# Windowed attention beside a channel MLP: which engine empties three PSUM tiles at the end of a pair of fill jobs

## The chip, the cores and the metric

The kernel runs on one core of one Trainium2 chip. The metric is the device time of one execution in microseconds (us). Before the change it is 768.82 us, the median of three runs (768.52 to 769.15).

## The reference, cut to what matters

```python
def _A_ref(x, wqkv, wo):                       # x: 1 x 2048 x 512, 32 heads of 16, window 256
    q, k, v = heads(x @ wqkv)
    scores = einsum("bhqd,bhkd->bhqk", q, k) * 16 ** -0.5
    scores = where((i >= j) & (i - j < 256), scores, -1e9)
    return merge(einsum("bhqk,bhkd->bhqd", softmax(scores), v)) @ wo
def _B_ref(x, w1, b1, w2, b2):                 # w1: 512 x 1792, w2: 1792 x 512
    return gelu(layernorm(x) @ w1 + b1) @ w2 + b2
xn = layernorm(x)
return x + _A_ref(xn, wqkv, wo) * silu(_B_ref(xn, w1, b1, w2, b2))
```

All of it is fp32. The projections and the MLP are made from a high and a low half of each operand, in three matmuls (`PASSES`).

## The kernel before

**The steps.** The 32 heads are worked on in 8 groups of 4, the 2048 tokens in 16 blocks of 128. One step `t` of the main loop (-16 to 128) works on block `t % 16` of group `t // 16`. The change touches steps 14 to 115. TensorE (PE) issues in each of these:

1. scores of four heads into the PSUM tile `stb`, first half (`prob_block(..., 1)`). ScalarE (ACT) takes their exponentials into a tile `pt`, and GpSimd (POOL) masks `pt`.
2. scores of the block that is 12 steps ahead, for its row maxima, into `xy` and, where the block has two blocks before it, into `zo` (`max_block`). VectorE (DVE) then merges `zo` into `xy` (COPY_PREDICATED) and reduces `xy` to the maxima `mt` (TENSOR_REDUCE).
3. some fill matmuls into the two PSUM tiles `fb0` and `fb1` (`fill_in(t, 0)`).
4. scores of the other half into `stb` (`prob_block(..., 0)`), and ACT's exponentials of these. `stb` is one tile, so this waits for the exponentials of item 1.
5. more fill matmuls (`fill_in(t, 1)`).
6. probabilities times values for the block of the step before, 12 narrow matmuls at most (24 in the profile, which has two rows for each), into `otb`, a quarter of the second bank of the tile `zo` (`pv_step`). `otb` is then copied to a quarter of the SBUF tile `oraw`. A full `oraw` goes to memory.

**The fill jobs.** Work that the later groups and the MLP need (the q and k projection of a group, the values' projection, the first MLP layer) runs as fills. `tandem` runs two such jobs at once through the two halves of TensorE's rows. One sums into `fb0`, the other into `fb1`, over steps `t0` to `t1`. In step `t1`, which this document calls a closing step, `fb0` is copied by ACT and `fb1` by DVE, into a tile `pjr` (projections), `vt` (values) or `hr` (MLP). The next pair starts in the next step and writes the same two tiles. There are 19 closing steps handled by the dictionary `closing`: 12 with `pjr`, 4 with `vt`, 3 with `hr`. (Pairs that end before step 9 or after step 115 go another way and are not touched.)

**The order.** `nc` is a wrapper that keeps each engine's instructions in the order in which the code issues them. So the order of the calls in the main loop is the order on every engine, and the engines meet through semaphores only. A tile is tracked as a whole where its PSUM bank is shared: the next step's scores into `zo` wait until `otb` has been copied.

```python
closing[t1] = (one[2], (fb[0], t1, nc.scalar.copy)), (two[2], (fb[1], t1, nc.vector.tensor_copy))   # L455, in tandem
```

Of the kernel before, what the change touches and what calls it, by code (L numbers as in the profile page):

```python
# [18 lines left out]
P = 128  # L19
# [30 lines left out]
def mixer_kernel(ctx, tc, x, wqk, wv, wo, w1, b1, w2, b2, out):  # L50


    nc = SimpleNamespace(**{name: Ordered(tc, name) for name in ("tensor", "vector", "scalar", "gpsimd", "sync")})
# [99 lines left out]
    def run(steps):  # L153
        for step in steps:
            step()
# [13 lines left out]
    def open_slot(i):  # L169
        slots.append(bigp.tile([P, 2, 2, S], F32R, tag=f"qk{i}", name=f"qk{i}"))  # L170
# [16 lines left out]
    otb = zo[:, 1, 256:384]  # L187
# [93 lines left out]
    closing = {}  # L281
# [191 lines left out]
    def max_block(n, qb):  # L473

        slot = slots[n % 2]
        if qb % 4 == 0:
            mts[n, qb // 4] = small.tile([P, 2, 2, 4], F32, tag="mt", name=f"mt_{n}_{qb}")
        lo = max(qb - 1, 0)
        off = 128 * (lo + 1 - qb)

        def scores(p, a, first):
            r = slice(64 * a, 64 * a + 64)
            out, keys = ((zo[:, a, P * p: P * (p + 1)], slice(P * (qb - 2), P * (qb - 1))) if first else
                         (xy[:, a, 256 * p + off: 256 * (p + 1)], slice(P * lo, P * (qb + 1))))
            nc.tensor.matmul(out, slot[r, 0, p, P * qb: P * (qb + 1)], slot[r, 1, p, keys], start=True, stop=True)

        for p, a, first in ((0, 1, False), (0, 0, False), (1, 1, False), (1, 0, False),
                            (0, 1, True), (0, 0, True), (1, 1, True), (1, 0, True)):
            if qb >= 2 or not first:
                scores(p, a, first)  # L490
        four = xy.rearrange("q a (p k) -> q a p k", p=2)
        nc.vector.copy_predicated(four[:, :, :, 128:256], mask,
                                  neg if qb < 2 else zo[:, :, 0:256].rearrange("q a (p k) -> q a p k", p=2))
        nc.vector.tensor_reduce(out=mts[n, qb // 4][:, :, :, qb % 4],
                                in_=four[:, :, :, off:256],
                                axis=AX.X, op=ALU.max, negate=True)

    def max_rows(n, c, t):

        mt = mts.pop((n, c))  # L500
        mh = small.tile([P, 2, 2, 2, 4], F32R, tag="mh", name=f"mh_{n}_{c}")
        nc.vector.tensor_copy(mh[:, :, 0], mt)
        nc.vector.tensor_sub(mh[:, :, 1], mt, mh[:, :, 0].bitcast(F32))
        mT = small.tile([P, 32], F32, tag="mT", name=f"mT_{n}_{c}")
        nc.vector.transpose(mT, mh.rearrange("p a l i b -> p (a l i b)").bitcast(F32))
        rows = mT_d[n, c]
        at(t + 1, nc.sync.dma_start, rows.rearrange("r (i t) -> i r t", i=4), mT)
        behind(t + 2, nc.sync.dma_start, slots[n % 2][3:P:32, 0, :, 512 * c: 512 * (c + 1)].bitcast(F32),
               rows.rearrange("(h p b) t -> h p (b t)", h=4, p=2))
# [4 lines left out]
    def prob_block(n, kb, p):  # L514
        slot = slots[n % 2]
        w = min(384, S - P * kb)
        pt = pp.tile([P, 2, 384], F32, tag="pt", name=f"pt_{n}_{kb}_{p}")
        both = xy if p and 16 * n + kb + LEAD >= 16 * NQ else stb[0]
        for a in (1, 0):
            r = slice(64 * a, 64 * a + 64)  # L520
            nc.tensor.matmul(both[:, a, 0:w], slot[r, 1, p, P * kb: P * (kb + 1)],
                             slot[r, 0, p, P * kb: P * kb + w], start=True, stop=True)
        nc.scalar.activation(pt[:, :, 0:w], both[:, :, 0:w], AF.Exp, scale=DH ** -0.5)
        nc.gpsimd.affine_select(out=pt[:, :, 0:P], in_=pt[:, :, 0:P], pattern=[[0, 2], [1, P]],
                                compare_op=ALU.is_ge, fill=0.0, base=0, channel_multiplier=-1)
        if w == 384:
            nc.gpsimd.affine_select(out=pt[:, :, 256:384], in_=pt[:, :, 256:384],
                                    pattern=[[0, 2], [-1, P]], compare_op=ALU.is_gt, fill=0.0,
                                    base=0, channel_multiplier=1)
        pts[(n, kb, p)] = pt  # L530


    outs = {}

    def pv_step(n, qb):

        lo = max(qb - 2, 0)
        for kb in range(lo, qb + 1):
            for j in range(4):
                nc.tensor.matmul(otb[32 * j: 32 * j + DH + 1], vt[:, kb, (4 * n + j) % 16],  # L540
                                 pts[n, kb, j // 2][:, j % 2, P * (qb - kb): P * (qb - kb + 1)],
                                 start=(kb == lo), stop=(kb == qb),
                                 skip_group_check=True, tile_position=(0, 32 * j))
        if qb % 4 == 0:
            outs[0] = sgp.tile([P, 512], F32, tag="or", name=f"oraw_{n}_{qb}", bufs=2)
        by = nc.vector.tensor_copy if 16 * n + qb + 1 in closing else nc.scalar.copy
        by(outs[0][:, P * (qb % 4): P * (qb % 4 + 1)], otb)
        if qb % 4 == 3:
            (at if n or qb > 7 else behind)(16 * n + qb + 2, nc.sync.dma_start, oT_d[n // 2, n % 2::2, :, P * (qb - 3): P * (qb + 1)], outs[0])

# [81 lines left out]
    def at(t, fn, *args):  # L632
        plan.setdefault(t, []).append((fn, args))
# [40 lines left out]
    n, raw = raws["qk"]  # L674
# [104 lines left out]
    def fill_in(t, half):  # L779
        now[:] = t, half  # L780
        run(delayed.pop((t, half), ()))
        for fn, args in fills.get((t, half), ()):
            fn(*args)

    end = 16 * NQ
    for t in range(-16, end + 1):
        m = t + LEAD
        if t == -5:
            open_slot(1)
            for k in range(4):  # L790
                at(-4 + k, clear_part, k)
        if 0 <= t < end:
            if t == 0:
                early.close()
                stb.append(attn.enter_context(tc.tile_pool(name="ps_s2", bufs=1, space=PSUM)).tile(
                    [P, 2, 512], F32, name="stb"))
            prob_block(t // 16, t % 16, 1)
        if t >= 0 and m < end:
            max_block(m // 16, m % 16)
        fill_in(t, 0)  # L800
        for fn, args in plan.get(t, []):
            fn(*args)
        if 4 <= m < LEAD:
            max_block(0, m)
        if 0 <= t < end:
            prob_block(t // 16, t % 16, 0)
        fill_in(t, 1)
        if 0 <= m < 4:
            max_block(0, m)
        if t >= 1:  # L810
            pv_step((t - 1) // 16, (t - 1) % 16)
        for fn, args in closing.get(t, ()):
            fn(*args)
        run(lns.get(t, ()))
        if 0 <= m < end and m % 4 == 3:
            max_rows(m // 16, m % 16 // 4, t)
        for fn, args in ends.get(t, []):
            fn(*args)
# [20 lines left out]
    for f in range(6, NF, 2):  # L839
        t = gp.tile([P, 2, 512], F32, tag="ohl", name=f"hr_{f}", bufs=4)  # L840
# [421 lines left out]
```

## Time and profile before

| what | value |
|---|---|
| median of three runs | 768.82 us |
| the profiled execution: its time, its span | 768.78 us, 767.1 us |
| granted TensorE clock | 0.999 |
| busy time of DVE, ACT, POOL | 529.1, 433.3, 292.6 us |
| copies of `otb` to `oraw` by ACT, by DVE | 109, 19 |
| steps that the change touches | between about 110 and 414 us of the span |

How to read it: "PE" is TensorE's matmuls, "PEld" its weight loads, which run ahead of the matmuls. [...] In the lists by time, the columns are the start and the duration in us, the engine, the line (the wrapper's line 42 for all), the operation, what it writes and reads, its shape, and in brackets the engine's idle time before it with what ended that. [...] In a row of a tile, three durations are the shortest, the median and the longest in ns.

### The profile page before, as it was taken

To read this page: it belongs to the slowest core of one execution; us is meant where nothing else is said; L and a number is where in the kernel's file an instruction comes from. 1 tells how busy PE (TensorE), PEld (TensorE's weight loads), DVE (VectorE), ACT (ScalarE), POOL (GpSimd) and SP (SyncE) were. 2 spreads that over 40 slices of the span, in tenths; PEclk is the share of its full clock that TensorE was granted. 3 is DMA by queue.
4 is the path that set the end of the run, shared out by engine and by line. 5 is a ranking of instruction groups with operands and counts; after the bars stand their busy time and mean duration, and the time that the engine had idled before them with its cause. 6 is when DMAs were issued, how large, how long until landed. Compare 5 with 4: busy or idle time off the path is not lost.

```text
span 767.1 us, 18795 instructions
## 1 busy us (share of the span) xinstructions
PE 746.9 (97%) x7428; PEld 583.6 (76%) x7428; DVE 529.1 (69%) x852; ACT 433.3 (56%) x723; POOL 292.6 (38%) x595
## 2 busy tenths in 40 slices
PE   9999999999999999999999999999999999999997
PEld 8777676666768887676676688888878888888886
DVE  6786777877777778897874447763657665676473
ACT  7736767867666666677776755444645553442001
POOL 7613556666565554766766800030101100001102
PEclk9999999999999999999999999999999999999999
DMA  7623455645447862455734283541202222253531
GB/s 261 207 45 78 94 133 138 153 112 134 95 100 227 241 199 98 113 147 144 201 111 152 61 289 121 180 151 54 70 29 93 99 87 84 77 165 116 173 96 55
DMA packets 56951, 99.40 MB, mean 130 GB/s; under 512 B 11104, under 2 KB 11360, under 8 KB 56864
## 3 DMA queue, kind: packets, MB, share of 16 engines
q1 hardware_dynamic: 56864, 98.21, 44.4%
q8 instruction: 58, 0.95, 0.5%
q14 instruction: 29, 0.24, 0.1%
HBM read 51.39 MB, written 29.62 MB: 106 GB/s over the span
## 4 chain that ended last, share of the span: by engine, by line
PE 81%; DVE 8%; issue 3%; ACT 3%; POOL 3%; DMA 2%; SPq 0%; DVEq 0%; ACTq 0%; POOLq 0%
PE acc L42 19%; PE fb L42 16%; PE zo L42 12%; PE p L42 9%; PE stb L42 6%; PE h L42 6%; PE s L42 6%; PE xy L42 4%; DVE xy L42 2%; DMA qk<-pjr 2%; PE pv L42 2%; ACT pt L42 2%; DVE mt L42 2%; POOL pt L42 1%; DVE pjr L42 1%
## 5 line engine op out<-in xcount | busy, mean ns | idle before, releaser
L42 POOL TENSOR_SCALAR_AFFINE_SELECT pt<-pt 128x256 f32<-128x256 f32 x480 | 193.2, 427 | 162.6 <-ACT pt L42 160.8
L42 ACT ACTIVATE pt<-stb 128x768 f32<-128x768 f32 (+1 forms) x244 | 188.6, 773 | 73.1 <-PE stb L42 64.9
L42 DVE TENSOR_REDUCE mt<-xy 128x4 f32<-128x1024 f32 (+1 forms) x128 | 152.6, 1192 | 4.4
L42 PE MATMUL acc<-w,gh 128*128 128x512 f32 x432 | 134.7, 393 | 0.0
L42 DVE COPY_PREDICATED xy<-upper,zo 128x512 f32<-128x512 int32 x112 | 77.5, 692 | 67.0 <-PE zo L42 66.5
L42 PE MATMUL fb<-xnT,wqb 64*128 64x512 f32 (+1 forms) x684 | 117.4, 406 | 2.9 <-DVE pjr L42 1.3
L42 PE MATMUL zo<-pt,vt 128*17 128x128 f32 x2880 | 103.7, 275 | 1.7 <-DVE xy L42 1.2
L42 POOL TENSOR_TENSOR xo<-xo,gated 128x512 f32<-128x512 f32 x15 | 20.2, 1348 | 219.1 <-DVE gated L42 214.2
L42 PE MATMUL stb<-qk 64*128 64x384 f32 (+1 forms) x488 | 95.5, 387 | 3.9 <-ACT pt L42 2.7
L42 PEld LDWEIGHTS zo<-pt,vt 128*17 128x17 f32 x2880 | 67.5, 97 | 38.3 <-DVE xy L42 18.9
L42 PEld LDWEIGHTS acc<-w,gh 128*128 128x128 f32 x432 | 80.9, 188 | 17.0
L42 PE MATMUL acc<-w,gl 128*128 128x512 f32 x216 | 84.3, 390 | 0.0
L42 PEld LDWEIGHTS stb<-qk 64*128 64x128 f32 x488 | 45.6, 183 | 45.7 <-ACT pt L42 34.2
L42 PEld LDWEIGHTS fb<-xnT,wqb 64*128 64x128 f32 (+1 forms) x684 | 63.7, 186 | 11.5 <-DVE pjr L42 3.3
L42 PE MATMUL xy<-qk 64*128 64x256 f32 (+2 forms) x536 | 62.9, 308 | 2.5 <-DVE mt L42 1.8
L42 PEld LDWEIGHTS xy<-qk 64*128 64x128 f32 x536 | 43.2, 185 | 15.5 <-DVE mt L42 6.8
L42 ACT COPY oraw<-zo 128x128 f32<-128x128 f32 x109 | 29.0, 266 | 36.0 <-PE zo L42 32.9
L42 PEld LDWEIGHTS acc<-w,gl 128*128 128x128 f32 x216 | 40.5, 188 | 9.6 <-DVE gl L42 0.5
L42 ACT ACTIVATE gated<-acc 128x512 f32<-128x512 f32 x16 | 8.7, 595 | 65.2 <-DVE acc L42 65.2
L42 PE MATMUL s<-wos,ohl 128*128 128x512 f32 (+1 forms) x204 | 44.8, 378 | 0.0
L42 PEld LDWEIGHTS s<-wos,ohl 128*128 128x128 f32 x204 | 36.7, 188 | 7.1
L42 ACT COPY p<-p 128x512 f32<-128x512 f32 x21 | 12.3, 585 | 50.1 <-PE p L42 42.6
(191 smaller groups left out, 1197.9 us busy)
## 6 DMA issues: line engine op xcount, KB each, us to landing
qk<-sh SPq DMA_DIRECT2D x128, 128.0 KB
qk<-pjr SPq DMA_DIRECT2D x64, 128.0 KB
oT_d<-oraw SPq DMA_DIRECT2D x32, 256.0 KB
w_d<-in_w_dram SPq DMA_DIRECT2D x14, 512.0 KB
x<-in_x_dram SPq DMA_DIRECT2D x16, 256.0 KB
or<-oT_d SPq DMA_DIRECT2D x16, 256.0 KB
w<-rden_d SPq DMA_DIRECT2D x16, 256.0 KB
xo<-in_x_dram SPq DMA_DIRECT2D x16, 256.0 KB
```

The source lines that it names most:

```text
L42: r = issue(*args, **kwargs)
```

## The change

In a closing step the copy of `otb` moves from DVE to ACT, and the two copies of the fill tiles are issued ahead of `pv_step` instead of behind it.

```diff
@@ pv_step
-        by = nc.vector.tensor_copy if 16 * n + qb + 1 in closing else nc.scalar.copy
-        by(outs[0][:, P * (qb % 4): P * (qb % 4 + 1)], otb)
+        nc.scalar.copy(outs[0][:, P * (qb % 4): P * (qb % 4 + 1)], otb)
@@ main loop
         fill_in(t, 1)
         if 0 <= m < 4:
             max_block(0, m)
+        for fn, args in closing.get(t, ()):
+            fn(*args)
         if t >= 1:
             pv_step((t - 1) // 16, (t - 1) % 16)
-        for fn, args in closing.get(t, ()):
-            fn(*args)
```

On VectorE in closing step 41 (around 191 us of the span), between this step's maxima and the next step's. `oraw` is the copy of `otb`, `pjr` the copy of `fb1`:

```order
 L42 COPY_PREDICATED xy<-upper,zo 128x4x128
 L42 TENSOR_REDUCE mt_4_2830<-xy 128x4
-L42 COPY oraw_8_2919<-zo 128x128
-L42 COPY pjr_3_2925<-fb_108 128x512
+L42 COPY pjr_3_2911<-fb_108 128x512
 L42 COPY_PREDICATED xy<-upper,zo 128x4x128
 L42 TENSOR_REDUCE mt_4_2830<-xy 128x4
```

VectorE's copy of `fb1` now stands directly behind the maxima, and one copy is gone. On ScalarE at the same place, between the second exponential of step 41 (`pt_9_0`) and the first of step 42 (`pt_10_1`):

```order
 L42 ACTIVATE pt_9_1_2875<-stb 128x768
 L42 ACTIVATE pt_9_0_2899<-stb 128x768
-L42 COPY pjr_2_2922<-fb_107 128x512
+L42 COPY pjr_2_2908<-fb_107 128x512
+L42 COPY oraw_8_2925<-zo 128x128
 L42 ACTIVATE pt_10_1_2930<-stb 128x768
 L42 ACTIVATE pt_10_0_2952<-stb 128x768
```

ScalarE's copy of `fb0` keeps its place, and the copy of `otb` comes between it and the next exponential. On VectorE in closing step 68 (around 271 us), one of the four with `vt`:

```order
 L42 COPY_PREDICATED xy<-upper,negc 128x4x128
 L42 TENSOR_REDUCE mt_0_4324<-xy 128x4
-L42 COPY oraw_0_4205<-zo 128x128
 L42 COPY vt<-fb_108 128x32x16
 L42 COPY_PREDICATED xy<-upper,negc 128x4x128
```

Here too one copy leaves VectorE and nothing else moves. TensorE, GpSimd and the DMA queue have the same instructions in the same order before and after. What changes there is whom TensorE's scores into `zo` wait for behind a closing step: ScalarE's copy of `otb` instead of VectorE's, in the 14 closing steps behind which there are such scores.

## The prediction

> **What bounds the kernel now.** I read the page's busy times first, then who waits for whom on TensorE's weight loads, then the tile `oraw`, and last the list by time around closing steps.
>
> ```profile
> PE 746.9 (97%) x7428; PEld 583.6 (76%) x7428; DVE 529.1 (69%) x852; ACT 433.3 (56%) x723; POOL 292.6 (38%) x595
> ```
>
> TensorE runs 97% of the span, so only time in which it is held counts. The waits of its weight loads show who holds it (us in total, times, longest):
>
> ```profile
> PEld stb L42 <- ACT pt L42: 34.2, 132, 1.3
> ...
> PEld fb L42 <- DVE pjr L42: 3.8, 11, 0.7
> PEld fb L42 <- DVE vt L42: 1.5, 4, 0.7
> ...
> PEld fb L42 <- DVE hr L42: 1.2, 3, 0.7
> ...
> PEld zo L42 <- ACT oraw L42: 0.5, 2, 0.3
> ```
>
> The three rows with `fb` are 18 waits, 6.5 us together, and they fall right behind 18 of the 19 closing steps: the next pair of jobs may not write `fb1` before VectorE has copied it. (Behind step 90 comes no pair but transposes, which are not in these rows.) The first row is the everyday limit: the second scores of a step wait for the exponential of the first.
>
> ```profile
> L42 ACT COPY oraw<-zo x109: 257/266/285, 73.3 to 445.1; 128x128 f32<-128x128 f32 x109
> ...
> L42 DVE COPY oraw<-zo x19: 278/290/292, 111.0 to 413.1; 128x128 f32<-128x128 f32 x19
> ```
>
> The 19 copies that leave VectorE take 290 ns each there; the same copy takes ScalarE 266 ns. Now one closing step, number 41, and the step behind it, first TensorE's weight loads:
>
> ```profile
> 190.96 0.57 PEld L42 LDWEIGHTS zo<-pt,vt 128*17 128x17 f32 x24 [0.30 <-DVE xy L42]
> ...
> 192.22 0.30 PEld L42 LDWEIGHTS zo<-qk 64*128 64x128 f32 x4
> 192.82 0.53 PEld L42 LDWEIGHTS fb<-xnT,wqb 64*128 64x128 f32 x6 [0.30 <-DVE pjr L42]
> 193.40 0.19 PEld L42 LDWEIGHTS stb<-qk 64*128 64x128 f32 x2
> ...
> 194.12 0.57 PEld L42 LDWEIGHTS zo<-pt,vt 128*17 128x17 f32 x24 [0.31 <-issue]
> ...
> 195.36 0.30 PEld L42 LDWEIGHTS zo<-qk 64*128 64x128 f32 x4
> 195.58 0.54 PEld L42 LDWEIGHTS fb<-xnT,wqb 64*128 64x128 f32 x6
> 196.34 0.18 PEld L42 LDWEIGHTS stb<-qk 64*128 64x128 f32 x2 [0.23 <-ACT pt L42]
> ...
> 196.95 0.34 PEld L42 LDWEIGHTS zo<-pt,vt 128*17 128x17 f32 x15 [0.31 <-DVE xy L42]
> ```
>
> From one product with the values to the next, 190.96 to 194.12 is 3.16 us and 194.12 to 196.95 is 2.83 us, with the same matmuls in both. The 0.33 us more lie between `zo` and `fb`: 0.60 us from 192.22 to 192.82 against 0.22 from 195.36 to 195.58. The other two engines in that place:
>
> ```profile
> 190.71 1.23 DVE L42 TENSOR_REDUCE mt<-xy 128x4 f32<-128x1024 f32 x1
> 191.88 0.29 DVE L42 COPY oraw<-zo 128x128 f32<-128x128 f32 x1
> 192.08 0.68 DVE L42 COPY pjr<-fb 128x512 f32<-128x512 f32 x1
> 192.70 0.69 DVE L42 COPY_PREDICATED xy<-upper,zo 128x512 f32<-128x512 int32 x1
> ```
>
> ```profile
> 190.84 0.81 ACT L42 ACTIVATE pt<-stb 128x768 f32<-128x768 f32 x1 [0.74 <-PE stb L42]
> 191.55 0.58 ACT L42 COPY pjr<-fb 128x512 f32<-128x512 f32 x1
> 192.31 0.81 ACT L42 ACTIVATE pt<-stb 128x768 f32<-128x768 f32 x1 [0.18 <-PE stb L42]
> ...
> 195.04 0.27 ACT L42 COPY oraw<-zo 128x128 f32<-128x128 f32 x1 [0.23 <-PE zo L42]
> 195.48 0.81 ACT L42 ACTIVATE pt<-stb 128x768 f32<-128x768 f32 x1 [0.17 <-PE stb L42]
> ```
>
> VectorE has no gap from the reduction (to 191.94) to the end of the bank's copy (192.76), and 0.06 us later TensorE loads for `fb`. So TensorE waits for VectorE's queue, not for data. ScalarE has 0.18 us to spare ahead of its next exponential.
>
> **The change, part by part.**
>
> *VectorE loses the copy of `otb`.* The bank's copy then starts where that copy started: 0.20 us earlier (192.08 less 191.88). The row of 290 ns is not the price, since neighbours overlap. Is `fb1` full by then? ScalarE copies `fb0`, whose last matmul is the neighbour of `fb1`'s last, from 191.55 on, so yes, with 0.33 us to spare. `fb` may now be loaded at 191.88 + 0.68 + 0.06 = 192.62 instead of 192.82, and the second `stb`, 0.58 us behind, at 193.20.
>
> *What is late next there.* Three things. First, the second `stb` needs the exponential of 192.31, which ends at 193.12; the gap from such an end to the load is 0.05 (195.48 + 0.81 = 196.29, load at 196.34). That gives 193.17, so 193.20 stands. Second, `zo` now waits for ScalarE's copy. Behind the bank's copy (191.55 + 0.58 = 192.13, less the 0.10 us by which 191.55 lies ahead of the end of the exponential, 190.84 + 0.81) it starts at 192.03 and ends at 192.30; the load of `zo` goes from 192.22 to about 192.35, and `fb` could follow 0.22 later, at 192.57: still ahead of 192.62. Third, VectorE's merge of `zo`, at 192.70 before, now waits for the later `zo` and comes about 0.1 us later; the reductions behind it have slack, since the next merge waits over a microsecond for TensorE.
>
> *ScalarE gains the copy of `otb`,* 266 ns in each of the 19 places. It can start only when the product with the values is done: 0.92 us after its first load (194.12 to 195.04), so at 191.88, while the bank's copy still runs. It ends at 192.30 and the exponential at 192.31 is not moved. If nothing overlapped, the copy would run from 192.13 to 192.40, the exponential would be 0.09 late, the second `stb` at 193.26, and the gain 0.14 us. I take 0.20, as the one pair of ScalarE's rows that stand back to back here overlaps, and keep 0.14 for the range.
>
> [...]
>
> *The same in the others.* Sixteen of the 18 waits have this form, a bank's copy that VectorE reaches behind a reduction and an `oraw`; at 0.20 us each they give 3.2 us. Two have longer waits, 0.66 us, because the block ahead has no scores in `zo` and a short reduction, so that VectorE waited for the values:
>
> ```profile
> 270.65 0.69 DVE L42 TENSOR_REDUCE mt<-xy 128x4 f32<-128x512 f32 x1
> ...
> 271.98 0.29 DVE L42 COPY oraw<-zo 128x128 f32<-128x128 f32 x1 [0.63 <-PE zo L42]
> 272.18 0.68 DVE L42 COPY vt<-fb 128x512 f32<-128x512 f32 x1
> 272.35 0.81 ACT L42 ACTIVATE pt<-stb 128x768 f32<-128x768 f32 x1 [0.18 <-PE stb L42]
> ...
> 272.92 0.77 PEld L42 LDWEIGHTS fb<-wva,xnT 64*128 64x128 f32 x12 [0.66 <-DVE vt L42]
> ...
> 273.62 0.19 PEld L42 LDWEIGHTS stb<-qk 64*128 64x128 f32 x2
> ```
>
> ```profile
> 321.48 0.81 ACT L42 ACTIVATE pt<-stb 128x768 f32<-128x768 f32 x1 [0.18 <-PE stb L42]
> ...
> 322.62 0.20 PEld L42 LDWEIGHTS stb<-qk 64*128 64x128 f32 x2
> ```
>
> Here VectorE's copy can start at about 271.3, and the whole wait goes. But then the second `stb` waits for the exponential: 272.35 + 0.81 + 0.05 = 273.21 instead of 273.62, a gain of 0.41 and not 0.66. In the other (321.48 + 0.86 = 322.34 against 322.62) it is 0.28. The nineteenth place, step 90, I put at nothing: no wait for a bank is removed, and a later `zo` costs 0.1 us at most.
>
> *The sum.* 16 x 0.20 + 0.41 + 0.28 = 3.9 us. Everything behind a closing step is in program order on every engine and hangs on TensorE, so it moves up as a whole, the 320 us of MLP at the end included. Against the profiled execution's 768.78 us (0.04 under the median) this gives 764.9 us.
>
> *The bounds.* On one side all 18 waits vanish and nothing takes their place: 6.5 us. On the other nothing is gained at `fb` and each of the 19 copies holds ScalarE's next exponential for its full 266 ns: 5.1 us lost. The sum is nearest to rows of the very place and I stay with it; its own range is 16 x 0.14 + 0.7 = 2.9 to about 5 us gained.
>
> **The rivals.**
>
> *A: the gain is waited out at the next gate.* In ordinary steps the second `stb` already waits for the exponential (34.2 us in 132 waits). My margin there is 0.03 us (193.17 against 193.20). If the moved copy delays the exponential by 0.17 us, from semaphores that no row prices, the second `stb` loads at 193.34, the gain in a place falls from 0.20 to 0.06, that of the two long waits to 0.24 and 0.11, and the sum to 16 x 0.06 + 0.35 = 1.3 us: 767.5 us, no change that counts. For it: the two waits of `zo` for ScalarE's `oraw`. Against it: at 195.04 and 195.48 that very copy stands ahead of an exponential, which waits for TensorE and not for the copy.
>
> *B: slower, by ScalarE's queue.* The copy waits for TensorE and the exponential stands behind it. Were the copy's end later than 192.30 by more than about 0.33 us, the exponential (0.10 ahead of that end) would start after 192.53 and the second `stb` come later than at 193.40. At 0.45 us later (a bank's copy that is slowed while VectorE copies too) each place loses 0.12 us: 2.3 us over 19, so 771.1 us. Against it: ScalarE's copy begins 0.3 us ahead of VectorE's and had VectorE's `oraw` beside it already.
>
> [...]
>
> *C: more than the sum.* VectorE has 19 x 0.29 = 5.5 us less to do, and if the reductions that TensorE's `xy` waits for also come earlier, all of the 6.5 us may go: 762.3 us. Against it: the exponential caps each place near the 0.2 us worked out.
>
> **How the numbers follow.** About 0.2% (1.5 us) is what a measurement of this kernel can tell from no change. The sum's case (2.5 to 5 us gained) has 0.63; a partial form of A, 1.5 to 2.5 us, 0.12; A in full, within 1.5 us, 0.15; B 0.05; C 0.05. So faster 0.80, same 0.15, slower 0.05. The forecast is 764.9 us; the range runs from 763.6 (a little of C) to 767.5 (A), which leaves out B and most of C.
>
> **What would show it.** In the new profile the rows of `fb` waiting for `pjr`, `vt` and `hr` should fall from 6.5 to about 2.5 us, closing step 41 should take 2.96 instead of 3.16 us, and VectorE's `oraw` rows should be gone. A is right if `stb` waiting for `pt` grows by about what `fb` loses; B if exponentials behind a closing step start later relative to the product with the values than 1.35 us (190.96 to 192.31). The forecast fails if copies on three PSUM tiles at once slow each other, which no row here shows.

## The result, and the profile after

The changed kernel takes 764.76 us (median of six runs, 764.48 to 765.04), beside 768.90 us for the kernel before (six runs, 768.52 to 769.34). The ratio is 0.9946 with a 95% interval of 0.9933 to 0.9958: faster by about 4.1 us. The forecast was 764.9 us in a range of 763.6 to 767.5. The profiled execution of the changed kernel took 764.76 us, its span is 763.0 us (767.1 before), and the granted clock is 0.999 in both, so the two traces can be compared directly.

First the busy times of the page of the changed kernel:

```profile
PE 746.3 (98%) x7428; PEld 583.1 (76%) x7428; DVE 525.7 (69%) x833; ACT 437.0 (57%) x742; POOL 293.0 (38%) x595
```

TensorE's work is the same; VectorE has 19 instructions fewer and ScalarE 19 more. The tile `oraw` now has one row, ScalarE's:

```profile
L42 ACT COPY oraw<-zo x128: 257/266/286, 73.2 to 441.2; 128x128 f32<-128x128 f32 x128
```

What TensorE's weight loads waited for (us in total, times, longest):

```profile
PEld stb L42 <- ACT pt L42: 35.8, 139, 1.3
...
PEld fb L42 <- DVE pjr L42: 0.6, 2, 0.3
PEld zo L42 <- ACT oraw L42: 0.5, 2, 0.3
...
PEld fb L42 <- DVE hr L42: 0.4, 1, 0.4
```

`fb` waiting for VectorE fell from 6.5 us in 18 waits to 1.0 us in three, and the row with `vt` is gone. The everyday wait of `stb` for the exponential grew by 1.6 us in seven more waits. `zo` waiting for `oraw` did not grow. Closing step 41 in the list by time, TensorE's loads, then VectorE, then ScalarE:

```profile
190.03 0.57 PEld L42 LDWEIGHTS zo<-pt,vt 128*17 128x17 f32 x24 [0.30 <-DVE xy L42]
...
191.42 0.30 PEld L42 LDWEIGHTS zo<-qk 64*128 64x128 f32 x4
191.65 0.53 PEld L42 LDWEIGHTS fb<-xnT,wqb 64*128 64x128 f32 x6
192.24 0.18 PEld L42 LDWEIGHTS stb<-qk 64*128 64x128 f32 x2
192.46 0.19 PEld L42 LDWEIGHTS fb<-xnT,wqb 64*128 64x128 f32 x2
192.95 0.57 PEld L42 LDWEIGHTS zo<-pt,vt 128*17 128x17 f32 x24 [0.31 <-DVE xy L42]
```

```profile
189.78 1.23 DVE L42 TENSOR_REDUCE mt<-xy 128x4 f32<-128x1024 f32 x1
190.92 0.68 DVE L42 COPY pjr<-fb 128x512 f32<-128x512 f32 x1
191.96 0.70 DVE L42 COPY_PREDICATED xy<-upper,zo 128x512 f32<-128x512 int32 x1 [0.36 <-PE zo L42]
```

```profile
189.91 0.81 ACT L42 ACTIVATE pt<-stb 128x768 f32<-128x768 f32 x1 [0.74 <-PE stb L42]
190.62 0.58 ACT L42 COPY pjr<-fb 128x512 f32<-128x512 f32 x1
191.09 0.29 ACT L42 COPY oraw<-zo 128x128 f32<-128x128 f32 x1
191.38 0.81 ACT L42 ACTIVATE pt<-stb 128x768 f32<-128x768 f32 x1
```

Counted from the product with the values (190.03), `zo` loads at 1.39, `fb` at 1.62 (1.86 before) with no wait in brackets, the exponential starts at 1.35 as before, and the next product comes at 2.92 instead of 3.16. Between `zo` and `fb` there are 0.23 us, the same as in a step that closes nothing (0.22).

All steps measured in this way, from one first load for the values to the next:

| closing steps | before to after, us | change in all |
|---|---|---|
| 16 ordinary ones (41: 3.16 to 2.92; 14: 3.59 to 3.38) | shorter by 0.13 to 0.30 each | -3.45 |
| 68 | 3.23 to 2.82 | -0.41 |
| 84 | 3.21 to 2.82 | -0.39 |
| 90 | 3.18 to 3.31 | +0.14 |
| all other steps together | | +0.20 |

In the chain of work that ended last, the MLP matmuls behind the loop, into the PSUM tile `acc`, begin at 444.08 instead of 448.00 us, 3.92 us earlier, which is the sum of the table but for roundings. The rest of the span moves with it; the 0.2 us by which the two spans differ beyond that is less than spans of one kernel differ among themselves (762.8 to 763.3 for the changed one).

### The profile page after: what moved, and what is told of

Its sections match the earlier page's. It is cut to its first block, busy times and chain, and to the rows that moved or that the text cites. A ratio compares the mean times of both kernels' runs of the same rounds, so it can differ in the third digit from the quotient of the medians.

```text
span 763.0 us, 18810 instructions
## 1 busy us (share of the span) xinstructions
PE 746.3 (98%) x7428; PEld 583.1 (76%) x7428; DVE 525.7 (69%) x833; ACT 437.0 (57%) x742; POOL 293.0 (38%) x595
## 4 chain that ended last, share of the span: by engine, by line
PE 86%; DVE 5%; ACT 3%; POOL 3%; issue 2%; DMA 1%; SPq 0%; ACTq 0%; DVEq 0%; POOLq 0%
PE acc L42 19%; PE fb L42 17%; PE zo L42 14%; PE p L42 9%; PE stb L42 8%; PE h L42 6%; PE s L42 6%; PE xy L42 5%; ACT pt L42 2%; PE pv L42 2%; DVE xy L42 1%; DVE mt L42 1%; POOL pt L42 1%; DVE xnT L42 1%; DMA oT_d<-oraw 1%
## 5 line engine op out<-in xcount | busy, mean ns | idle before, releaser
L42 ACT COPY oraw<-zo 128x128 f32<-128x128 f32 x128 | 34.3, 268 | 36.5 <-PE zo L42 33.6
```

Of the source, the lines that this page charges most:

```text
L42: r = issue(*args, **kwargs)
```

## The experiments

The theory: TensorE stood behind VectorE's queue at `fb1`, so each place gains the time by which VectorE reaches its bank copy earlier, 0.20 us, as long as ScalarE's copy delays neither the exponential nor `zo`. The rivals: the gain is waited out at the second `stb` (A), or ScalarE's queue costs more than VectorE's (B).

**Each half alone.** In the first kernel ScalarE copies `otb`, but the bank copies stay behind `pv_step`. In the second only the order is changed, so that VectorE still copies `otb`, now behind its bank copy.

```diff
 first, in pv_step
-        by = nc.vector.tensor_copy if 16 * n + qb + 1 in closing else nc.scalar.copy
-        by(outs[0][:, P * (qb % 4): P * (qb % 4 + 1)], otb)
+        nc.scalar.copy(outs[0][:, P * (qb % 4): P * (qb % 4 + 1)], otb)
 second, in the main loop
+        for fn, args in closing.get(t, ()):
+            fn(*args)
         if t >= 1:
             pv_step((t - 1) // 16, (t - 1) % 16)
-        for fn, args in closing.get(t, ()):
-            fn(*args)
```

> One part alone: in closing steps ScalarE copies otb (as in the changed kernel), but both bank copies stay behind pv_step, as before. Theory (both halves are needed: the gain comes from VectorE's queue, but ScalarE's bank copy must be out of the way before the values are done): VectorE's bank copy comes 0.2 us earlier, but ScalarE's queue is now otb's copy (0.92 us after the values' first load) and then the bank's (0.58 us), so the next step's first exponential starts at about 1.58 instead of 1.35 us and the second stb at about 2.44 us, where it stood before. Only places with short exponentials, or where stb stood later than that, gain: about 1.5 us in all, 767.3 us (766.8 to 767.9). Rival (only what VectorE no longer does counts): 764.8 us, as the changed kernel.

Measured: 766.24 us (766.04 to 766.70), ratio 0.9966 (0.9953 to 0.9978). That is 2.6 us faster than before: more than the theory's 1.5 us and just outside its range, and less than the rival's 4.1 us. ScalarE in step 41, and TensorE's loads and the matmul of the second `stb` there:

```profile
191.54 0.27 ACT L42 COPY oraw<-zo 128x128 f32<-128x128 f32 x1 [0.22 <-PE zo L42]
191.70 0.59 ACT L42 COPY pjr<-fb 128x512 f32<-128x512 f32 x1
192.18 0.83 ACT L42 ACTIVATE pt<-stb 128x768 f32<-128x768 f32 x1
```

```profile
190.62 0.57 PEld L42 LDWEIGHTS zo<-pt,vt 128*17 128x17 f32 x24 [0.30 <-DVE xy L42]
...
193.06 0.19 PEld L42 LDWEIGHTS stb<-qk 64*128 64x128 f32 x2 [0.19 <-ACT pt L42]
```

```profile
193.06 0.44 PE L42 MATMUL stb<-qk 64*128 64x384 f32 x2
```

The exponential is late as expected (192.18 is 1.56 behind the values), and the second `stb` waits for it (192.18 + 0.83 + 0.05 = 193.06). Its load is at 2.44, exactly where it was before (193.40 less 190.96). Yet the step is 0.12 shorter. The reason is in a row of the kernel before that the prediction did not look at, the matmul that belongs to that load:

```profile
193.62 0.34 PE L42 MATMUL stb<-qk 64*128 64x384 f32 x2
```

It came 0.22 us behind its weight load, at 2.66; in the experiment load and matmul stand together at 2.44. But the row of the matmul whose load has waited is also longer, 0.44 instead of 0.34 us, so the two starts can't be compared. The ends can: the matmul ended at 3.00 before (193.62 + 0.34 less 190.96) and ends at 2.88 here (193.06 + 0.44 less 190.62). These 0.12 us are what the step gains. (The profile models the ends of matmuls. They can be used here, as the next product follows this end by 0.16 us in step 41 before the change, 193.96 to 194.12, and by 0.17 us here, 193.50 to 193.67.) In the changed kernel the end is at 2.76, again 0.16 us ahead of the next product:

```profile
192.46 0.33 PE L42 MATMUL stb<-qk 64*128 64x384 f32 x2
```

So before the change the load had about 0.12 us of slack, which the expectation counted as a limit.

> The other part alone: the bank copies stand ahead of pv_step, but VectorE still copies otb in closing steps, now behind its bank copy. Theory: fb1 is free 0.2 us earlier, but otb's copy ends at about 1.84 us after the values' first load instead of 1.2, and the next step's scores into zo wait for it: zo loads at about 1.89 instead of 1.31 us and fb 0.22 us behind, at 2.11 instead of 1.88. Ten places lose 0.23 us, two 0.12, step 90 0.4, step 53 gains 0.1; the five places without scores in zo (19, 35, 68, 84, 115) gain 1.4 us together. Sum 1.4 us slower: 770.3 us (769.6 to 771.0). Rival (an early bank copy is all that counts): 764.8 us.

Measured: 770.06 us (769.58 to 771.08), ratio 1.0015 (1.0006 to 1.0025): 1.2 us slower, as expected. VectorE and TensorE's loads in step 41, and the wait that appears:

```profile
192.61 0.68 DVE L42 COPY pjr<-fb 128x512 f32<-128x512 f32 x1
193.20 0.28 DVE L42 COPY oraw<-zo 128x128 f32<-128x128 f32 x1
```

```profile
193.54 0.30 PEld L42 LDWEIGHTS zo<-qk 64*128 64x128 f32 x4 [0.49 <-DVE oraw L42]
193.75 0.53 PEld L42 LDWEIGHTS fb<-xnT,wqb 64*128 64x128 f32 x6
```

```profile
PEld zo L42 <- DVE oraw L42: 6.8, 14, 0.5
```

The waits of `fb` are down to the 1.0 us of the changed kernel, but in the 14 closing steps with scores behind them in `zo` the next scores wait for the copy of `otb`, which is now last in the queue. Here the order paid only with the other engine.

**The price of a copy in the queue.** A second copy of `otb`, into a tile that nothing reads, put behind the first: on VectorE in the kernel before, and on ScalarE in the changed kernel.

```diff
+    spare = sgp.tile([P, P], F32, tag="spare", name="spare", bufs=1)
 on VectorE, in before           # by(...) of otb stands above
+        if 16 * n + qb + 1 in closing:
+            by(spare, otb)
 on ScalarE, in the changed one  # nc.scalar.copy(...) of otb stands above
+        if 16 * n + qb + 1 in closing:
+            nc.scalar.copy(spare, otb)
```

> The doubled copy on VectorE once more, with a second copy that does not wait for the first: in the kernel before, the second copy of otb in a closing step goes to a spare tile. In the earlier doubling both wrote one place, and the profile had 0.52 us from the first copy to the bank's instead of 0.20, so the second waited for the first to end. Theory (an independent copy in VectorE's queue costs 0.20 us, from start to start, and all of it lies on TensorE's path in 18 places): 0.20 more in each, 3.6 to 3.9 us, 772.6 us (772.0 to 773.2). Rival (any second copy costs 0.32 us, as in the earlier doubling): 775.8 us.

Measured: 772.74 us (772.27 to 772.97), ratio 1.0048 (1.0033 to 1.0063), as expected. All 19 closing steps are longer, by 0.17 to 0.23 us, 3.70 us together, or 0.195 each. VectorE in step 41:

```profile
193.54 0.29 DVE L42 COPY oraw<-zo 128x128 f32<-128x128 f32 x1
193.75 0.28 DVE L42 COPY spare<-zo 128x128 f32<-128x128 f32 x1
193.95 0.68 DVE L42 COPY pjr<-fb 128x512 f32<-128x512 f32 x1
```

From start to start these copies take 0.21 and 0.20 us, and that is what TensorE pays for one.

> The same on ScalarE in the changed kernel: the second copy of otb in a closing step goes to a spare tile and need not wait for the first. In the earlier doubling the next exponential started 0.18 us later (1.53 instead of 1.35 us after the values' first load) and zo 0.30 later (1.69 instead of 1.39). Theory (an independent copy takes about 0.2 us of ScalarE's queue, and the moved copy had left less than 0.1 us of room): the exponential moves by about 0.1 us and zo by about 0.2 in the places where ScalarE's bank copy ends last; 1.0 to 2.2 us slower than the changed kernel, 766.4 us (765.8 to 767.0). Rival (the loss of the earlier doubling was only the wait of one copy for the other): 764.8 us.

Measured: 765.68 us (765.58 to 765.83), ratio to the kernel before 0.9958 (0.9941 to 0.9975). That is 0.9 us slower than the changed kernel by the medians, or 1.15 us if each is taken against its own runs of the kernel before (2.99 and 4.14 us gained), and just below the theory's range. ScalarE and one of TensorE's loads in step 41:

```profile
190.53 0.58 ACT L42 COPY pjr<-fb 128x512 f32<-128x512 f32 x1
190.99 0.28 ACT L42 COPY oraw<-zo 128x128 f32<-128x128 f32 x1
191.15 0.30 ACT L42 COPY spare<-zo 128x128 f32<-128x128 f32 x1
191.31 0.86 ACT L42 ACTIVATE pt<-stb 128x768 f32<-128x768 f32 x1
```

```profile
189.94 0.57 PEld L42 LDWEIGHTS zo<-pt,vt 128*17 128x17 f32 x24 [0.30 <-DVE xy L42]
...
191.50 0.30 PEld L42 LDWEIGHTS zo<-qk 64*128 64x128 f32 x4 [0.24 <-ACT spare L42]
```

The start of the exponential moved from 1.35 to 1.37 only, though 0.16 us of copy had been added: ScalarE had about 0.14 us of room in front of it. In the changed kernel it starts 0.29 us behind the start of the last copy (191.09 to 191.38), and here 0.16 us (191.15 to 191.31). Its row is also longer here, 0.86 instead of 0.81 us, so its end moved by 0.07 us. What gave way was `zo`, from 1.39 to 1.56. Six steps with a late `zo` (41, 53, 58, 74, 90, 98) are 0.16 to 0.17 longer, 68 and 84 by 0.05 to 0.07, the others by nothing; 1.05 us together. So what limits next is `zo` in these six steps, and the exponential in 68 and 84.

**The copy doubled onto the same place.** An earlier form of these two, in which the second copy writes the same quarter of `oraw` as the first.

```diff
 on VectorE, in before
+        if 16 * n + qb + 1 in closing:
+            by(outs[0][:, P * (qb % 4): P * (qb % 4 + 1)], otb)
 on ScalarE, in the changed one
+        if 16 * n + qb + 1 in closing:
+            nc.scalar.copy(outs[0][:, P * (qb % 4): P * (qb % 4 + 1)], otb)
```

> The suspected cost doubled: the kernel before, but in the 19 closing steps VectorE copies otb twice, one copy behind the other, ahead of its bank copy. Theory (the price is the time from one start to the next, 0.20 us, and all of it lies on TensorE's path): 18 places lose 0.20 us each, 3.6 us, 772.5 us (771.9 to 773.1). Rival 1 (the price is the copy's own row, 0.29 us, in 19 places): 5.5 us, 774.4 us. Rival 2 (the copy was hidden and the gain came from elsewhere): 768.9 us.

Measured: 775.84 us (775.43 to 776.01), ratio 1.0092 (1.0078 to 1.0106), 7.0 us slower, which is more than the theory and both rivals allowed. They took 0.29 us at most for the second copy. VectorE in step 14:

```profile
111.42 0.60 DVE L42 COPY oraw<-zo 128x128 f32<-128x128 f32 x2
111.94 0.68 DVE L42 COPY pjr<-fb 128x512 f32<-128x512 f32 x1
```

The two copies take 0.52 us from the first's start to the next instruction's, where two with separate targets take 0.41 (193.54 to 193.95 above). Writing the same place, the second waits for the first: in the program of this kernel the first copy signals a semaphore (number 100) for which the second waits, in all 19 places, and with separate targets the second copy waits for none. So this run doubles more than was meant: 17 places lost 0.31 to 0.34 us, 19 and 98 lost 0.60 and 0.55. What the last two lost beyond the others is not explained.

> The added cost doubled: the changed kernel, but ScalarE copies otb twice in each of the 19 closing steps, one copy behind the other. It measures how much room there is behind the moved copy. Theory (one copy just fits: the margin of the next exponential is 0.0 to 0.1 us): in the 11 places where ScalarE's bank copy ends last, the second copy ends at about 1.5 us after the values' first load, the exponential and zo move by about 0.17 us; in the other 8 by 0 to 0.05: 2.1 us slower than the changed kernel, 766.9 us (766.2 to 767.6). Rival 1 (ScalarE has room to spare): 764.8 us. Rival 2 (every copy on ScalarE costs its whole row, 0.27 us in 19 places): 5.1 us, 769.9 us, and then the first copy would have cost as much.

Measured: 767.53 us (766.81 to 768.15), ratio 0.9982 (0.9973 to 0.9991), inside the range. ScalarE and one of TensorE's loads in step 41, and the wait:

```profile
192.09 0.58 ACT L42 COPY oraw<-zo 128x128 f32<-128x128 f32 x2
192.58 0.82 ACT L42 ACTIVATE pt<-stb 128x768 f32<-128x768 f32 x1
```

```profile
192.73 0.30 PEld L42 LDWEIGHTS zo<-qk 64*128 64x128 f32 x4 [0.36 <-ACT oraw L42]
```

```profile
PEld zo L42 <- ACT oraw L42: 3.4, 11, 0.4
```

Here too the pair takes 0.49 us, where separate targets take 0.32 (190.99 to 191.31). The cost is again at `zo` (0.5 to 3.4 us), not at the exponential alone, which the separate-target run then showed cleanly.

**Two places, and all but one.** A function `moved(t)` selects, for both halves of the change, the steps in which it applies: only 68 and 84, or all but 90.

```diff
+    def moved(t):
+        return t in (68, 84)        # second kernel: t != 90
```

> The change in closing steps 68 and 84 alone, where VectorE waited for the values before it could copy the bank; the other 17 as before. Theory: the second stb there comes as early as the exponential lets it, both steps last 2.82 us instead of 3.23 and 3.21: 0.8 us gained, 768.1 us. By the prediction's term (0.41 and 0.28) 768.2 us; only the profile can tell these apart, by step 84 (2.82 or 2.93 us). It also shows whether the 0.33 us that step 83 lost in the changed kernel, a wait for a transfer, belongs to the other places: if so step 83 still lasts 3.15 us.

Measured: 768.03 us (767.46 to 768.43), ratio 0.9989 (0.9980 to 0.9998): 0.8 us, as expected. Steps 68 and 84 take 2.82 and 2.81 us, as in the changed kernel, so a place's gain does not depend on the other places. Step 83 takes 2.96 us, neither the 3.15 of before nor the 2.82 of the changed kernel, so what the run was to say of it stays open. Step 84:

```profile
319.27 0.57 PEld L42 LDWEIGHTS zo<-pt,vt 128*17 128x17 f32 x24 [0.30 <-issue]
...
321.48 0.19 PEld L42 LDWEIGHTS stb<-qk 64*128 64x128 f32 x2 [0.46 <-ACT pt L42]
...
322.08 0.57 PEld L42 LDWEIGHTS zo<-pt,vt 128*17 128x17 f32 x24 [0.31 <-issue]
```

The second `stb` is at 2.21 and waits for the exponential; the prediction had it at 2.20.

> The changed kernel with closing step 90 as before. Theory: step 90 went from 3.18 to 3.31 us because its later zo holds the transposes and no wait for a bank is removed there; it comes back to 3.18 us, and the whole is 0.1 us faster than the changed kernel at most (764.6 us), which a time can't tell. Rival: step 90 got longer for what came before it, and stays at 3.31 us.

Measured: one run, 765.34 us, which tells nothing at this size. The trace does: step 90 takes 3.17 us again instead of 3.31, and `zo` loads 1.27 us behind the values instead of 1.39. The loss of 0.14 us in step 90 is thus the price of ScalarE's later copy where no wait for a bank was there to be removed.

**The other bank first.** In the changed kernel the last limit of an ordinary closing step could still be the order of the two fill tiles, since the next pair writes `fb1` first. Here `fb0`, which ScalarE empties earlier, comes first in the first half of a pair.

```diff
-                    (two if phase == 0 else one)[1](fb[1 - phase], i, hi, **flags)
-                    (one if phase == 0 else two)[1](fb[phase], i, lo, **flags)
+                    if phase == 0:
+                        one[1](fb[0], i, lo, **flags)
+                        two[1](fb[1], i, hi, **flags)
+                    else:
+                        one[1](fb[0], i, hi, **flags)
+                        two[1](fb[1], i, lo, **flags)
```

> A version that may beat the changed kernel: of each two fill matmuls of a pair's first half, the one into fb0 is issued first instead of the one into fb1, in all pairs. Behind a closing step ScalarE frees fb0 at about 1.2 us after the values' first load, VectorE fb1 only at 1.62 to 1.7. Theory: the first fb load moves up to 0.22 us behind zo, and where zo is early (six places, 1.31 us) and in steps 24 and 104 the rest follows about 0.09 us earlier: 0.5 us gained, 764.3 us, about as much as can be told. Rival (fb1 holds the pair in any case, since the second matmul stands right behind): 764.8 us.

Measured: 764.89 us (764.64 to 765.15), ratio to the kernel before 0.9951 (0.9937 to 0.9965), no different from the changed kernel. In step 14 `fb` is loaded 1.54 us behind the values instead of 1.67, and the step still takes 3.36 us instead of 3.38: the gain is waited out at the neighbour `fb1`. No version that was run beats the changed kernel.

## Why the prediction was right

- **What bounds the kernel.** Right: TensorE was held by VectorE's queue at `fb1`. A copy added to that queue costs 0.195 us a place, one taken away gives 0.216 (3.45 / 16), for the reason two points below.
- **The price of VectorE's copy.** 0.20 us from start to start (191.88 to 192.08 in step 41 before the change), and not the row's 0.29: the two rows overlap by 0.09 us there, and the added copy cost 0.195 us a place.
- **Sixteen ordinary places, 3.2 us.** Mis-sized by 0.25: they gave 3.45. The forecast took all sixteen as places in which VectorE's queue has no gap. In six of them (35, 41, 53, 58, 74 and 115) the copy of `otb` had also waited for the values, and the bank copy lost that wait too. These gave 0.24 to 0.30 us each; the other ten gave 0.13 to 0.22, 0.19 on average, which is the price of the copy. In step 41 the wait was about 0.03 us: the bank copy came 0.23 us earlier relative to the values (from 1.12 to 0.89), `fb` was loaded at 1.62 instead of the 1.66 forecast, and the step took 2.92 instead of 2.96. In step 53 the bank copy came 0.56 us earlier, and the later `zo` held the gain to 0.30.
- **Step 68, 0.41 us.** Right to the hundredth, and limited by the exponential as forecast. The forecast went by the weight load of before (273.62), and here that load stood only 0.11 us ahead of its matmul, so little was lost by it. ScalarE and TensorE there:

```profile
270.66 0.81 ACT L42 ACTIVATE pt<-stb 128x768 f32<-128x768 f32 x1
```

```profile
271.52 0.19 PEld L42 LDWEIGHTS stb<-qk 64*128 64x128 f32 x2 [0.23 <-ACT pt L42]
```

- **Step 84, 0.28 us.** Mis-sized: 0.39. The forecast of the second `stb`'s load was right (2.20; 2.21 measured), but the gain was taken against the weight load of before (322.62), which stood 0.23 us ahead of its matmul. That matmul before, and with only 68 and 84 changed:

```profile
322.85 0.34 PE L42 MATMUL stb<-qk 64*128 64x384 f32 x2
```

```profile
321.48 0.44 PE L42 MATMUL stb<-qk 64*128 64x384 f32 x2
```

  Counted from the values (320.14 and 319.27) it ended at 3.05 and 2.65: 0.40 us, where the loads give 0.28 and the starts of the two rows 0.50. The step went from 3.21 to 2.81.

- **Step 90, nothing.** It lost 0.14 us. The mechanism, a later `zo`, was named; its price was put at 0.1 us at most and then left out of the sum.
- **The waits of `fb`, about 2.5 us left.** Only 1.0 us is left in the list, in steps 19, 35 and 115, which have no scores in `zo` behind them. In steps 41, 53, 58, 74 and 98 `fb` now follows `zo` with no wait at all. In the other eight ordinary steps it still waits for 0.05 to 0.07 us, which the list, counting from 0.15 us on, leaves out. Of the 1.6 us by which `stb` waits longer for `pt`, 0.7 us are in steps 68 and 84, where the exponential took over.
- **The sum.** 3.9 us was forecast, and the closing steps gave 4.12. The errors of +0.25, +0.11 and -0.14 account for the difference. That the time was met to 0.14 us is partly luck: these errors cancel in part, and the other steps took 0.2 us back.
- **The other steps** were put at nothing, and four of them changed by more than 0.1 us. Step 83 is 0.33 us shorter. It takes 2.81 or 2.82 us in the six kernels in which ScalarE copies `otb` in every closing step (in one of them in all but step 90), and 2.88 to 3.27 in the other five, so it goes with the change; what ended its longer wait is not shown. Step 48 is 0.17 longer: its scores into `xy` wait 0.29 instead of 0.11 us for VectorE's maxima, whose reduction starts 3.02 us behind the values of step 47 where it started at 3.00. So the 0.15 us that closing step 47 gained were waited out one step later, as rival A has it, but at another gate. Step 55 is 0.28 longer, in two other variants of the changed kernel too and in none of the other seven experiments; why is open. Step 11 is 0.11 longer, ahead of the first closing step, so the change does not explain it.
- **Rival A** did not happen: the exponential starts at 1.35 as before. The run with ScalarE's separate second copy shows why: the exponential had about 0.14 us of slack ahead of it. The second `stb`, where the prediction saw a margin of 0.03 us, had more too: in the first experiment the matmul whose load had waited ended 0.44 us behind that load (2.44 and 2.88). From this I estimate that its load could have come at 2.32 instead of 2.21 without a later end than the 2.76 of step 41. **Rival B** neither. In all 19 closing steps of the changed kernel the exponential follows ScalarE's copy, 0.24 to 0.59 us from start to start. The wrapper keeps this order in the program, so no run could have shown another. In step 41 the copy starts 1.06 us behind the values and the exponential at 1.35, as before, so there the copy cost it nothing. **C** is excluded by 764.48 as the lowest run.

## What to carry to other kernels

When TensorE waits for a PSUM tile, look what stands in front of the emptying copy on its engine, and price that by the distance from start to start (here 0.20 us, where the row has 0.29). Moving the neighbour to the other engine paid here only in part without the new order, and the new order not at all without the move: the engine alone gained 2.6 us, the order alone lost 1.2 us, and both together gained 4.1 us. Read what a wait costs on the end of the matmul and not on its weight load, which ran ahead by 0.22 us in step 41 and by 0.23 us in step 84 before the change: in step 84 the load moved by 0.28 us, and the matmul's end, like the step, by 0.40.

## What was not expected of the hardware

- Two copies on one engine to the same place were further apart than two to separate places: 0.52 against 0.41 us for the pair on VectorE, 0.49 against 0.32 on ScalarE. The programs of the two kernels with one place have the second copy wait for a semaphore that the first signals (100 on VectorE, 102 on ScalarE); what the engines would do without that wait was not measured. On VectorE the doubled copy cost 0.195 us a place with a target of its own, and 0.31 to 0.34 us in 17 places without.
- The weight load's row of the second `stb` started 0.22 us (193.40 and 193.62) and 0.23 us (322.62 and 322.85) ahead of its matmul's in steps 41 and 84 before the change, while the rows of matmuls into `fb` still ran. Where that load waited for the exponential, in step 41 of the first experiment (193.06) and in step 84 with only 68 and 84 changed (321.48), both rows start together, and the matmul's row is longer by 0.10 us (0.44 against 0.34).
- Back to back with separate targets, the copy of 128x128 took ScalarE 0.16 us from start to start (190.99, 191.15, 191.31), less than VectorE's 0.20, though its rows were as long (0.28 and 0.30 against 0.29 and 0.28).
